# One PSUM ring for attention and FFN, and RMS weights folded into the FFN weights one group earlier

## The chip, the cores and the metric

The kernel runs on one core of one Trainium2 chip. The metric is the device time of one execution in microseconds (us), the median of several runs. Five engines work side by side, each through its own list of instructions in order: PE (matmuls, with weight loads shown as PEld), DVE, ACT, POOL, and SP, which issues transfers. POOL issues transfers as well. PE writes its results only to PSUM, which has eight banks of 128 x 512 float32 values; DVE and ACT read them from there, POOL does not.

## The reference

Inputs are q, k, v of 8 batches x 8 heads x 576 tokens x 64, a forget gate f of 8 x 8 x 576, and the FFN's weights.

```python
scores = scale * np.matmul(q, k.transpose(0, 1, 3, 2))
cum = np.cumsum(np.log(np.clip(f, 0.0001, 1.0)), axis=-1)
scores = np.where(causal, -1e9, scores + cum[..., :, None] - cum[..., None, :])
x = softmax(scores) @ v            # heads side by side: 4608 tokens x 512
xn = x / np.sqrt(np.mean(x * x, axis=-1, keepdims=True) + 1e-06) * rms_g
g = xn @ w_gate                    # 512 x 1536
out = (g * sigmoid(g) * (xn @ w_val)) @ w_out   # 1536 x 512
```

## The kernel before, in words

**Attention.** Each batch has five query blocks `qi`: four of 128 tokens and a last one (`LAST`) of 64. Queries and keys are loaded as bf16 by POOL (`load_qk`, L302; `load_qk2`, L308, for 256 tokens at once), values as float32 by POOL or SP (`load_v`, L319). Queries and keys must be turned so that the head dimension lies on the partitions: by transposing transfers on SP (`turn`, L378), or for most blocks of batches 0 and 1 by PE into a PSUM bank, emptied by DVE for q and ACT for k (`turn_pe`, L387). Values are multiplied by the decay of their key (`scale_v`, L418; L426 and L427), on DVE for batches 0 and 1, on POOL for the others.

A score tile is one query block against one key block (or two key blocks for `LAST`): eight matmuls (L451) into two PSUM banks, even heads in one and odd heads in the other. `score_block` (L439) takes two tiles at a time. ACT takes the exponential of both banks of a tile in one instruction (L469), and POOL masks the diagonal tile (L476). The score blocks form a chain in the fixed order of the list `order` (L565): blocks 0 to 3 of batch 0, those of batch 1, `LAST` of batch 0, `LAST` of batch 1, and then batch after batch. `values` (L485) multiplies probabilities with values (L498) for even and for odd heads, each into one bank, and DVE divides by the sum and moves the result to SBUF (L512, L514). `norm` (L521) squares (ACT, L530), takes the power -0.5 (POOL, L534 and L535) and scales (ACT, L542). The result is turned again: for groups 0 and 1 by PE (L550), and DVE moves it to `xT` and multiplies by the RMS weights `rgT` on the way (L556); for the other groups by a transposing transfer on SP (L560), without the multiplication.

**FFN.** A group is 512 tokens: groups 0 to 7 are the first 512 of each batch, group 8 the eight `LAST` blocks together. `gate` (L596) computes 512 columns' worth of gate and value matmuls (L605) in one bank each, then tanh on ACT (L617) and two instructions on DVE, L619 (which frees the gate bank) and L612 (which frees the value bank). Groups 0 and 1 run by pieces: one gate takes four 128-wide chunks of the hidden dimension for 128 tokens, so a block `i` of the weights (512 of the 1536 columns) is used by four gates, one for each piece `j`. Later groups take one chunk for all 512 tokens, with four matmuls of 512 columns. `project` (L624) multiplies with `w_out` (L630), in three units of four matmuls into one bank, which ACT empties (L635) and SP stores (L638).

**The RMS weights.** Since groups 0 and 1 multiply xT by `rgT` while the others do not, the weights `wg` and `wv` are multiplied by `rgT` in SBUF between groups 1 and 2. `weigh` (L339) does so for one block of each, with four instructions on DVE for wg and four for wv (L345), and has to wait until the four gates of group 1 have used the block; group 2's gates wait for it.

**The order of the work.** The program is not scheduled by hand. Each piece of work is a `Unit` with an engine, an estimated duration, a `key` and the buffers that it takes and gives back (`Hold`). `Plan.run` (L79) simulates the engines with these durations and lets each idle engine take, of its units that are ready and whose buffers are free (`fits`, L54), the one with the lowest key; a small random number from a fixed seed is added to each key (L88). The resulting order is what each engine executes. The group number is the FFN's key: gates of group g have keys from g to g + 0.69, its projections from g + 1.03. `akey` (L235) gives the attention of batch b from 2 on keys from b - 1.3 to b - 0.45; batches 0 and 1 have negative keys (`qkey`, L569). The due times of `load` at L663 hold loads of batches 2 and later back until certain gates have begun.

**PSUM.** Three rings share the eight banks: `sc`, two slots of two banks, for scores; `po`, one bank, for values; `ff`, three banks, for turns, gates, projections and the odd heads of batch 0's values. When the last score (or value) has been planned, its slots pass to `ff` (`heir`, L69). Rings not named in the set at L207 are handed out to whichever unit runs first, and `sc`, `po` and `ff` are not named there.

Of the kernel before, what the change touches and what calls it, by code (L numbers as in the profile page):

```python
# [32 lines left out]
class Plan:  # L33
# [3 lines left out]
    def __init__(self, rings, fifo, heir):  # L37
        self.units, self.fifo, self.heir = [], fifo, heir
        self.free = {name: list(range(n)) for name, n in rings.items()}
        self.left = {name: [] for name in rings}  # L40
# [106 lines left out]
def fox_ffn_kernel(ctx, tc, q, k, v, f, moe_w_gate, moe_w_val, moe_w_out, moe_rms_g, out):  # L147
# [15 lines left out]
    def ring(name, n, shape, dt, pool=sb):  # L163
# [3 lines left out]
                 sc=2, po=1, ff=3, hw=8, sw=8)  # L167
# [38 lines left out]

    P = Plan(sizes, {"v32", "qk", "qk2", "QT", "Vs", "PT", "x", "xn"}, {"sc": ("ff", lambda i: [n_ff + 2 * i, n_ff + 2 * i + 1]),  # L207
                     "po": ("ff", lambda i: [n_ff + 2 * n_sc + i])})
# [25 lines left out]

    def akey(b, w):  # L235
        return b - 1 - LEAD + SPAN * w
# [20 lines left out]
    iden_f = pool(0.7, -15.5, emit_ident)  # L257
# [20 lines left out]
    h_dec = Hold("ff", 1 + EARLY)  # L278

    def emit_dect():  # L280
        for j in range(NB):
            nc.tensor.transpose(T_ff[h_dec.slot][:, j * 64:(j + 1) * 64], dec[:, j * 128:(j + 1) * 128],
                                ident_f[0:BH, 0:BH])
# [3 lines left out]
        decT, T_ff[h_dec.slot][:, 0:NB * 64].rearrange("p (j b) -> p j b", b=BH)), [d5], give=[h_dec])  # L287
# [44 lines left out]
    def load_w(i, key):  # L332
        c0, c1 = i * 512, (i + 1) * 512
        for w, src, nm in ((wg, moe_w_gate, "g"), (wv, moe_w_val, "v")):
            def emit(w=w, src=src):
                nc.gpsimd.dma_start(out=w[:, :, c0:c1], in_=src[:, c0:c1].rearrange("(c p) f -> p c f", p=128))
            Lw[nm, i] = load("POOL", 0.75, (512, 0.0061), key, emit, late=2.6)

    def weigh(i, key, deps):  # L339

        c0, c1 = i * 512, (i + 1) * 512
        for w, nm in ((wg, "g"), (wv, "v")):
# [3 lines left out]
            Lw[nm, i] = dve(1.14, key, emit, deps)  # L346
# [40 lines left out]
    def turn_pe(b, j, two, key):  # L387

        t0, r_of = j * 128, 2 if two else 1
        for dst, nm, add, cp in ((T_QT, "q", dve, nc.vector.tensor_copy), (T_KT, "k", act, nc.scalar.copy)):  # L390
            hq, h = hold_qk[b, nm, j], Hold("ff", 1)

            def emit(hq=hq, h=h):
                tp = T_ff[h.slot].bitcast(BF16)
# [12 lines left out]
            def copy(dst=dst, h=h, cp=cp):  # L407
                tp = T_ff[h.slot].bitcast(BF16)[:, 0:512 * r_of].rearrange("p (c r t) -> p c r t", r=r_of, t=128)
# [9 lines left out]
    def scale_v(b, j, key):  # L418
# [3 lines left out]
        def emit(eng):  # L422
            dj = decT[0:n, j, b * H:(b + 1) * H]
            if early:
                dj = T_ff[h_dec.slot][0:n, j * 64:j * 64 + H]
# [10 lines left out]

    hold_PT, masked, last_block = {}, {}, [None]

    def score_block(tiles, key):  # L439

        holds = [Hold("sc", 1) for _ in tiles]

        def emit():
            for (b, qi, kjs, n), h in zip(tiles, holds):
                kt, qt, t = T_KT[hold_QT[b].slot], T_QT[hold_QT[b].slot], T_sc[h.slot]
# [12 lines left out]
        u = pe(0.19 + 0.24 * cols, key, emit, deps, take=holds, give=gives)  # L458
        last_block[0] = u
        for (b, qi, kjs, n), h in zip(tiles, holds):  # L460
# [7 lines left out]
            def ex(h=h, hp=hp, cols=cols, T_of_p=T_of_p, half=half):  # L468
                nc.scalar.activation(T_of_p[hp.slot][:, 0:2 * half].rearrange("p (a c) -> p a c", a=2)[:, :, 0:cols],  # L469
                                     T_sc[h.slot][:, :, 0:cols], ACT.Exp, scale=scale)  # L470
            e = act(0.2 + 0.82 * cols / 512, key, ex, [u], take=[hp], give=[h])
# [8 lines left out]
    def bank_of(h):  # L480
        return T_ff[h.slot] if h.ring == "ff" else T_po[h.slot]

    hold_x, evac, last_val = {}, {}, [None]

    def values(b, qi, key):  # L485
        p0, n = rows(qi)
        hx = hold_x[b, qi] = Hold("x", 1)
        for par in range(2):
            hpo = Hold("ff" if b == 0 and par == 1 and qi < LAST else "po", 1)

            def emit(par=par, hpo=hpo):
                po = bank_of(hpo)[:, 0:4 * 65].rearrange("p (j d) -> p j d", d=65)
# [16 lines left out]
            def ev(par=par, hpo=hpo):  # L509
                po = bank_of(hpo)[0:n, 0:4 * 65].rearrange("p (j d) -> p j d", d=65)  # L510
# [10 lines left out]
    def norm(b, js, key):  # L521
# [15 lines left out]
        for i, j in enumerate(js):  # L537
# [6 lines left out]
            if g < 2:  # L544
                hf = Hold("ff", 1)

                def tr(hn=hn, hf=hf):
                    tp = T_ff[hf.slot].bitcast(BF16)
# [5 lines left out]
                def cp(hf=hf, g=g, c=c):  # L554
                    tp = T_ff[hf.slot].bitcast(BF16)[:, 0:512].rearrange("p (c t) -> p c t", t=128)
                    nc.vector.tensor_tensor(T_of[g][hold_xT[g].slot][:, :, c:c + 128], tp, bcast(rgT, 128), ALU.mult)  # L556
                pieces[b, j] = dve(0.65, key - 0.02, cp, [t, L_rg], take=[hold_xT[g]], give=[hf])
# [38 lines left out]
    def gate(g, key, deps, i, pairs):  # L596

        hg, hv, ht, ha = Hold("ff", 1), Hold("ff", 1), Hold("th", 1), Hold("ga", 1)
        hx = hold_xT[g]

        def mm(w, h):
            xT = T_of[g][hx.slot]
            for fc, t0, n, c in pairs:
                for dc in range(NDC):
                    nc.tensor.matmul(T_ff[h.slot][:, c:c + n], lhsT=w[:, dc, fc * 128:(fc + 1) * 128],  # L605
                                     rhs=xT[:, dc, t0:t0 + n], start=(dc == 0), stop=(dc == NDC - 1))

        def last():
            fc, t0, n, c = pairs[0]
            hT = T_hT[hold_hT[g].slot][:, fc:fc + len(pairs), t0:t0 + n]  # L610
            three = [t.rearrange("p (f t) -> p f t", t=n) for t in (T_ga[ha.slot], T_ff[hv.slot])]
# [5 lines left out]
        th = act(0.6, key - 0.1, lambda: nc.scalar.activation(T_th[ht.slot], T_ff[hg.slot], ACT.Tanh, scale=0.5),  # L617
                 [ug], take=[ht])
        a = dve(0.72, key - 0.1, lambda: nc.vector.scalar_tensor_tensor(  # L619
            T_ga[ha.slot], in0=T_th[ht.slot], scalar=1.0, in1=T_ff[hg.slot], op0=ALU.add, op1=ALU.mult),  # L620
# [3 lines left out]
    def project(g, j, key):  # L624
        hf, ho = Hold("ff", 1), Hold("ores", 1)
        last = None
        for part in range(3):
            def emit(part=part):
                for fc in range(part * 4, part * 4 + 4):
                    nc.tensor.matmul(T_ff[hf.slot], lhsT=T_hT[hold_hT[g].slot][:, fc, j * 128:(j + 1) * 128],  # L630
# [4 lines left out]
        c = act(0.59, key - 0.05, lambda: nc.scalar.copy(T_ores[ho.slot], T_ff[hf.slot]), [last], take=[ho], give=[hf])  # L635
# [12 lines left out]
    for g in range(G):  # L648
        if g < 2:
            for i in range(3):  # L650
# [4 lines left out]
                if g == 1:  # L655
                    weigh(i, 1 + (i * 4 + 4) / 16, [ended[1, i * 4 + j] for j in range(4)])
# [54 lines left out]
```

## Time and profile before

| | |
|---|---|
| median of 3 runs | 400.06 us (399.75 to 400.39) |
| profiled execution | 398.83 us |
| its span, first to last instruction | 396.7 us |
| mean granted TensorE clock | 0.984 |
| PE, DVE, ACT, POOL busy | 92%, 57%, 60%, 50% of the span |
| moved | 44.83 MB |

A row of the profile names line, engine, operation, `out<-in` by the names of the program's tiles with buffer numbers left out, shapes and the count. In rows of groups, the first number behind the bar is busy time in us and the second the mean duration of one in ns; what follows is idle time of the engine just before them and what ended it. In the timeline the first two numbers are start and duration in us, and the bracket holds the idle time before and what ended it. In rows of waits, "a <- b" says that a waited for b, in us in total, how many times, and the longest. A busy PE is not a PE at its peak, since the ends of matmuls are modelled.

### The profile page before, as it was taken

Reading aid. Unit: us, or ns where it says so; the run is one execution under the profiler, and the core shown is the slowest. Engines: PE = TensorE matmul, PEld = TensorE weight load, DVE = VectorE, ACT = ScalarE, POOL = GpSimd, SP = SyncE. Lnnn points to the kernel's source line nnn. Section 1 sums busy time; section 2 is a strip of 40 time slices with the busy share of each in tenths; the row PEclk is TensorE's granted clock in tenths of the full one; section 3 lists DMA queues with packets and bytes.
Section 4 is the critical chain, followed back from the end, with each engine's and each line's share of the span. In section 5 each row is a group of like instructions: output and inputs, shape, how many; then the busy total and the mean of one; then the engine's idle time right before and its main releaser. Section 6 shows DMA issues by size and latency. Waiting matters only on the chain.

```text
span 396.7 us, 9672 instructions
## 1 busy us (share of the span) xinstructions
PE 365.8 (92%) x3941; PEld 217.4 (55%) x3941; DVE 225.0 (57%) x456; ACT 237.7 (60%) x377; POOL 196.8 (50%) x275
## 2 busy tenths in 40 slices
PE   2668999997699999899999999999999999999995
PEld 1567898785496554554455544554555444444442
DVE  4555787478968555564565555645555554455530
ACT  4655588786647955786677657865885532232212
POOL 8862469997839945695398456841211100000000
PEclk9998999999979999999999999999999999999998
DMA  9999999999829999899799999992120210001004
GB/s 132 189 200 190 199 143 162 176 175 168 141 39 109 187 158 122 103 154 154 78 122 168 161 112 82 190 150 55 32 57 28 55 33 28 26 26 55 26 28 106
DMA packets 133708, 44.83 MB, mean 113 GB/s; under 512 B 122432, under 2 KB 127040, under 8 KB 133664
## 3 DMA queue, kind: packets, MB, share of 16 engines
q0 software_dynamic: 76000, 22.16, 59.2%
q1 hardware_dynamic: 57136, 22.05, 30.7%
q8 instruction: 31, 0.51, 0.6%
q10 hardware_dynamic: 528, 0.00, 0.2%
q14 instruction: 13, 0.11, 0.1%
HBM read 37.90 MB, written 9.44 MB: 119 GB/s over the span
## 4 chain that ended last, share of the span: by engine, by line
PE 78%; DMA 7%; DVE 7%; POOL 4%; issue 2%; ACT 1%; SPq 0%; ACTq 0%; POOLq 0%
PE ff L605 35%; PE ff L630 17%; PE po L498 7%; PE sc L605 6%; PE sc L451 6%; PE sc L630 5%; DMA v<-in_v_dram 4%; DMA xT<-xn 3%; PE po L605 2%; DVE wg L345 1%; DVE wv L345 1%; DVE hT L612 1%; DVE ga L619 1%; POOL qk L303 1%; DVE x L514 1%
## 5 line engine op out<-in xcount | busy, mean ns | idle before, releaser
L469 ACT ACTIVATE PT<-sc 128x1024 bf16<-128x1024 f32 x96 | 95.2, 1018 | 22.6 <-PE sc L451 22.5
L605 PE MATMUL ff<-xT,wg 128*128 128x128 bf16 (+1 forms) x628 | 88.8, 290 | 5.9 <-DVE ga L619 3.2
L605 PE MATMUL ff<-xT,wv 128*128 128x128 bf16 (+1 forms) x636 | 90.7, 288 | 1.0 <-DVE hT L612 0.8
L619 DVE SCALAR_TENSOR_TENSOR ga<-th,ff 128x512 f32<-128x512 f32 x87 | 59.2, 683 | 49.2 <-ACT th L617 48.8
L630 PE MATMUL ff<-wo,hT 128*128 128x512 bf16 x336 | 86.1, 379 | 0.0
L605 PEld LDWEIGHTS <-wg 128*128 128x128 bf16 x720 | 55.9, 102 | 42.4 <-issue 6.3
L617 ACT ACTIVATE th<-ff 128x512 f32<-128x512 f32 x87 | 51.5, 595 | 44.6 <-PE ff L605 32.8
L605 PEld LDWEIGHTS <-wv 128*128 128x128 bf16 x720 | 54.9, 100 | 36.6 <-issue 1.8
L612 DVE SCALAR_TENSOR_TENSOR hT<-ga,ff 128x512 bf16<-128x512 f32 x94 | 63.7, 683 | 18.7 <-PE ff L605 16.7
L630 PEld LDWEIGHTS <-hT 128*128 128x128 bf16 x432 | 40.1, 98 | 45.1 <-issue 1.3
L476 POOL TENSOR_SCALAR_AFFINE_SELECT PT<-PT 128x1024 bf16<-128x1024 bf16 x32 | 35.4, 1106 | 58.0 <-ACT PT L469 57.7
L498 PEld LDWEIGHTS <-PT 128*128 128x128 bf16 x896 | 38.4, 99 | 17.3 <-issue 4.8
L498 PE MATMUL po<-Vs,PT 128*128 128x65 bf16 x856 | 41.1, 196 | 3.2 <-DVE x L514 2.4
L426 POOL TENSOR_TENSOR Vs<-v,decT 128x512 bf16<-128x512 f32 (+1 forms) x30 | 31.7, 1057 | 12.8 <-DMA v<-in_v_dram 12.2
L451 PE MATMUL sc<-QT,KT 64*128 64x128 bf16 (+1 forms) x960 | 34.6, 214 | 3.0 <-ACT PT L469 1.4
L512 DVE RECIPROCAL rden<-po 128x4 f32<-128x4 f32 (+1 forms) x76 | 13.5, 177 | 40.7 <-PE po L498 40.5
L451 PEld LDWEIGHTS <-KT 64*128 64x128 bf16 x960 | 25.0, 97 | 19.4 <-issue 14.9
L530 ACT ACTIVATE junk<-x 128x512 bf16<-128x512 f32 (+1 forms) x40 | 25.1, 627 | 14.7 <-DVE x L514 14.6
L514 DVE TENSOR_TENSOR x<-po,rden 128x256 f32<-128x256 f32 (+1 forms) x76 | 32.1, 423 | 2.6
L326 POOL DMA_DIRECT2D v<-in_v_dram x34 | 30.4, 896 | 0.1
L303 POOL DMA_DIRECT2D qk<-in_q_dram x34 | 30.1, 885 | 0.8 <-POOLq L695 0.8
L542 ACT ACTIVATE xn<-x,rs 128x512 bf16<-128x512 f32 (+1 forms) x40 | 27.2, 714 | 5.4 <-POOL rs L535 5.3
(76 smaller groups left out, 306.1 us busy)
## 6 DMA issues: line engine op xcount, KB each, us to landing
out_dram<-ores SPq DMA_DIRECT2D x32, 256.0 KB, 2.4
v<-in_v_dram POOLq DMA_DIRECT2D x27, 256.0 KB, 5.3
qk<-in_q_dram POOLq DMA_DIRECT2D x26, 128.0 KB, 5.9
qk<-in_k_dram POOLq DMA_DIRECT2D x26, 128.0 KB, 5.7
wg<-in_moe_w_gate_dram POOLq DMA_DIRECT2D x3, 512.0 KB, 15.9
wv<-in_moe_w_val_dram POOLq DMA_DIRECT2D x3, 512.0 KB, 17.4
wo<-in_moe_w_out_dram POOLq DMA_DIRECT2D x2, 768.0 KB, 17.6
v<-in_v_dram SPq DMA_DIRECT2D x5, 256.0 KB, 9.9
```

What stands on the lines that cost most here:

```text
L303: nc.gpsimd.dma_start(out=T_qk[h.slot][0:n, :].rearrange("p (h d) -> p h d", d=D), in_=src[b, :, p0:p0 + n, :].rearrange("h p d -> p h d"))
L426: eng.tensor_tensor(T_Vs[hv.slot][0:n, j, :, 0:D], T_v32[h.slot][0:n, :, :], bcast(dj, D), ALU.mult)
L451: nc.tensor.matmul(t[:, par, c:c + n], lhsT=kt[r, p, kj * 128:(kj + 1) * 128], rhs=qt[r, p, qi * 128:qi * 128 + n], start=True, stop=True)
L469: nc.scalar.activation(T_of_p[hp.slot][:, 0:2 * half].rearrange("p (a c) -> p a c", a=2)[:, :, 0:cols], T_sc[h.slot][:, :, 0:cols], ACT.Ex ...
L476: nc.gpsimd.affine_select(out=d, in_=d, pattern=[[0, 8], [1, n]], compare_op=ALU.is_ge, fill=0.0, base=0, channel_multiplier=-1)
L498: nc.tensor.matmul(po[:, p, :], lhsT=T_of_p[h.slot][:, c:c + 128], rhs=vs[:, kj, 2 * p + par, :], start=(kj == 0), stop=(kj == qi))
L514: nc.vector.tensor_tensor(d, po[:, :, 0:D], bcast(r, D), ALU.mult)
L605: nc.tensor.matmul(T_ff[h.slot][:, c:c + n], lhsT=w[:, dc, fc * 128:(fc + 1) * 128], rhs=xT[:, dc, t0:t0 + n], start=(dc == 0), stop=(dc = ...
L612: nc.vector.scalar_tensor_tensor(hT, in0=three[0], scalar=0.5, in1=three[1], op0=ALU.mult, op1=ALU.mult)
L617: th = act(0.6, key - 0.1, lambda: nc.scalar.activation(T_th[ht.slot], T_ff[hg.slot], ACT.Tanh, scale=0.5), [ug], take=[ht])
L619: a = dve(0.72, key - 0.1, lambda: nc.vector.scalar_tensor_tensor(T_ga[ha.slot], in0=T_th[ht.slot], scalar=1.0, in1=T_ff[hg.slot], op0=ALU ...
L630: nc.tensor.matmul(T_ff[hf.slot], lhsT=T_hT[hold_hT[g].slot][:, fc, j * 128:(j + 1) * 128], rhs=wo[:, fc, :], start=(fc == 0), stop=(fc == ...
```

## The change

All eight banks become one tile `banks` and one ring `bank`, for scores, values, turns, projections and gates alike. A score tile takes any two banks, and its view steps from the lower to the higher of them. The rule of inheritance goes, as do the three rings.

Group 0 alone is multiplied by `rgT` in xT (`PLAIN = 1`); group 1's pieces are copied. `weigh` runs between groups 0 and 1: wg of a block once the four gate halves of group 0 on it are done, wv once the value halves are. All gates from group 1 on wait for the weighed block. The key of the weighing is 0.25 below that of the first gate which needs it, and its estimated duration is 1.3 us for four instructions instead of 1.14.

The identity matrix for PE's transposes is made on POOL behind the loads of key -15 instead of ahead of them. The attention of the `LAST` blocks of batches 0 and 1 gets keys 0.3 and 0.9 instead of -4.8 and -4.2. The seed of the small random numbers is 5 instead of 71.

The core of the diff (the replacement of `T_ff`, `T_po` and `T_sc` by `T_bank` in `turn_pe`, `gate`, `project`, `norm` and at the decay's transpose is left out):

```diff
@@ Plan
-                if h.ring in self.heir and not self.left[h.ring]:
-                    to, slots = self.heir[h.ring]
-                    self.free[to] += slots(h.slot)
-                else:
-                    self.free[h.ring].append(h.slot)
+                self.free[h.ring].append(h.slot)
...
-        draw = random.Random(71)
+        draw = random.Random(5)
@@ fox_ffn_kernel
-                 sc=2, po=1, ff=3, hw=8, sw=8)
+                 bank=8, hw=8, sw=8)
...
-    T_sc = ring("sc", sizes["sc"], [128, 2, 512], F32, ps)
-    T_po = ring("po", sizes["po"], [128, 512], F32, ps)
-    T_ff = ring("ff", sizes["ff"], [128, GT], F32, ps)
-    n_ff, n_sc = sizes["ff"], sizes["sc"]
-    T_ff += [t[:, i, :] for t in T_sc for i in range(2)] + T_po
+    banks = ps.tile([128, sizes["bank"], 512], F32, name="banks")
+    T_bank = [banks[:, i, :] for i in range(sizes["bank"])]
...
+    PLAIN = 1
...
-    iden_f = pool(0.7, -15.5, emit_ident)
+    iden_f = pool(0.7, -14.5, emit_ident)
@@ weigh
-            Lw[nm, i] = dve(1.14, key, emit, deps)
+            Lw[nm, i] = [dve(1.3, key, emit, deps[nm])]
@@ score_block
+    def two_banks(h):
+        a, z = sorted(x.slot for x in h)
+        return banks[:, a:z + 1:z - a, :]
...
-        holds = [Hold("sc", 1) for _ in tiles]
+        holds = [(Hold("bank", 1), Hold("bank", 1)) for _ in tiles]
...
-                                     T_sc[h.slot][:, :, 0:cols], ACT.Exp, scale=scale)
+                                     two_banks(h)[:, :, 0:cols], ACT.Exp, scale=scale)
@@ values
-            hpo = Hold("ff" if b == 0 and par == 1 and qi < LAST else "po", 1)
+            hpo = Hold("bank", 1)
@@ norm
-                    nc.vector.tensor_tensor(T_of[g][hold_xT[g].slot][:, :, c:c + 128], tp, bcast(rgT, 128), ALU.mult)
-                pieces[b, j] = dve(0.65, key - 0.02, cp, [t, L_rg], take=[hold_xT[g]], give=[hf])
+                    to = T_of[g][hold_xT[g].slot][:, :, c:c + 128]
+                    if g < PLAIN:
+                        nc.vector.tensor_tensor(to, tp, bcast(rgT, 128), ALU.mult)
+                    else:
+                        nc.vector.tensor_copy(to, tp)
+                pieces[b, j] = dve(0.69 if g < PLAIN else 0.42, key - 0.02, cp, [t, L_rg], take=[hold_xT[g]], give=[hf])
@@ qkey
-            return (2 * b - 9 + 0.2 * (START[qi] + ahead)) if qi < LAST else -4.8 + 0.6 * b + 0.04 * ahead
+            return (2 * b - 9 + 0.2 * (START[qi] + ahead)) if qi < LAST else 0.3 + 0.6 * b + 0.04 * ahead
@@ gate
-        began[g, len([x for x in began if x[0] == g])] = ug = pe(dur, key, lambda: mm(wg, hg), deps + [Lw["g", i]], take=[hg])
-        uv = pe(dur, key + 0.0001, lambda: mm(wv, hv), [ug, Lw["v", i]], take=[hv], give=[hx])
+        began[g, len([x for x in began if x[0] == g])] = ug = pe(dur, key, lambda: mm(wg, hg), deps + Lw["g", i], take=[hg])
+        uv = pe(dur, key + 0.0001, lambda: mm(wv, hv), [ug] + Lw["v", i], take=[hv], give=[hx])
@@ groups
-                if g == 1:
-                    weigh(i, 1 + (i * 4 + 4) / 16, [ended[1, i * 4 + j] for j in range(4)])
+                if g == PLAIN - 1:
+                    weigh(i, PLAIN - 1 + (i * 4 + 12) / 16, {"g": [began[g, i * 4 + j] for j in range(4)],
+                                                            "v": [ended[g, i * 4 + j] for j in range(4)]})
```

More of the change, by code (lines that the diff above doesn't have):

```diff
@@ L277, in fox_ffn_kernel @@
     EARLY = 3
-    h_dec = Hold("ff", 1 + EARLY)
+    h_dec = Hold("bank", 1 + EARLY)
     def emit_dect():
         for j in range(NB):
-            nc.tensor.transpose(T_ff[h_dec.slot][:, j * 64:(j + 1) * 64], dec[:, j * 128:(j + 1) * 128],
+            nc.tensor.transpose(T_bank[h_dec.slot][:, j * 64:(j + 1) * 64], dec[:, j * 128:(j + 1) * 128],
                                 ident_f[0:BH, 0:BH])
@@ L286, in fox_ffn_kernel @@
     L_dec = dve(0.45, -19, lambda: nc.vector.tensor_copy(
-        decT, T_ff[h_dec.slot][:, 0:NB * 64].rearrange("p (j b) -> p j b", b=BH)), [d5], give=[h_dec])
+        decT, T_bank[h_dec.slot][:, 0:NB * 64].rearrange("p (j b) -> p j b", b=BH)), [d5], give=[h_dec])
     def rows(j):
@@ L336, in emit @@
                 nc.gpsimd.dma_start(out=w[:, :, c0:c1], in_=src[:, c0:c1].rearrange("(c p) f -> p c f", p=128))
-            Lw[nm, i] = load("POOL", 0.75, (512, 0.0061), key, emit, late=2.6)
+            Lw[nm, i] = [load("POOL", 0.75, (512, 0.0061), key, emit, late=2.6)]
     def weigh(i, key, deps):
@@ L390, in turn_pe @@
         for dst, nm, add, cp in ((T_QT, "q", dve, nc.vector.tensor_copy), (T_KT, "k", act, nc.scalar.copy)):
-            hq, h = hold_qk[b, nm, j], Hold("ff", 1)
+            hq, h = hold_qk[b, nm, j], Hold("bank", 1)
             def emit(hq=hq, h=h):
-                tp = T_ff[h.slot].bitcast(BF16)
+                tp = T_bank[h.slot].bitcast(BF16)
                 for p in range(4):
@@ L457, in score_block @@
         cols = sum(len(kjs) * n / 128 for b, qi, kjs, n in tiles)
-        u = pe(0.19 + 0.24 * cols, key, emit, deps, take=holds, give=gives)
+        u = pe(0.19 + 0.24 * cols, key, emit, deps, take=[x for h in holds for x in h], give=gives)
         last_block[0] = u
@@ L469, in ex @@
                 nc.scalar.activation(T_of_p[hp.slot][:, 0:2 * half].rearrange("p (a c) -> p a c", a=2)[:, :, 0:cols],
-                                     T_sc[h.slot][:, :, 0:cols], ACT.Exp, scale=scale)
-            e = act(0.2 + 0.82 * cols / 512, key, ex, [u], take=[hp], give=[h])
+                                     two_banks(h)[:, :, 0:cols], ACT.Exp, scale=scale)
+            e = act(0.2 + 0.82 * cols / 512, key, ex, [u], take=[hp], give=h)
             masked.setdefault((b, qi), []).append(e)
@@ L478, in score_block @@
                 masked[b, qi].append(pool(0.15 + 0.95 * n / 128, key, mk, [e]))
-    def bank_of(h):
-        return T_ff[h.slot] if h.ring == "ff" else T_po[h.slot]
     hold_x, evac, last_val = {}, {}, [None]
@@ L544, in norm @@
             if g < 2:
-                hf = Hold("ff", 1)
+                hf = Hold("bank", 1)
                 def tr(hn=hn, hf=hf):
-                    tp = T_ff[hf.slot].bitcast(BF16)
+                    tp = T_bank[hf.slot].bitcast(BF16)
                     for dc in range(NDC):
@@ L596, in gate @@
     def gate(g, key, deps, i, pairs):
-        hg, hv, ht, ha = Hold("ff", 1), Hold("ff", 1), Hold("th", 1), Hold("ga", 1)
+        hg, hv, ht, ha = Hold("bank", 1), Hold("bank", 1), Hold("th", 1), Hold("ga", 1)
         hx = hold_xT[g]
@@ L624, in project @@
     def project(g, j, key):
-        hf, ho = Hold("ff", 1), Hold("ores", 1)
+        hf, ho = Hold("bank", 1), Hold("ores", 1)
         last = None
@@ L634, in project @@
                       give=[hold_hT[g]] if part == 2 else [])
-        c = act(0.59, key - 0.05, lambda: nc.scalar.copy(T_ores[ho.slot], T_ff[hf.slot]), [last], take=[ho], give=[hf])
+        c = act(0.59, key - 0.05, lambda: nc.scalar.copy(T_ores[ho.slot], T_bank[hf.slot]), [last], take=[ho], give=[hf])
         if g < B:
```

29 lines of the change are left out of this document (14 added, 15 removed).

## The prediction, as it was recorded

> **What bounds the kernel now.** First the page's busy times and its chain, then busy time by stage (columns: length of the stretch, then PE, PEld, DVE, ACT, POOL busy us with instruction counts, the granted TensorE clock, DMA share, GB/s).
>
> ```profile
> PE 365.8 (92%) x3941; PEld 217.4 (55%) x3941; DVE 225.0 (57%) x456; ACT 237.7 (60%) x377; POOL 196.8 (50%) x275
> PE 78%; DMA 7%; DVE 7%; POOL 4%; issue 2%; ACT 1%; SPq 0%; ACTq 0%; POOLq 0%
> ```
> ```profile
> 0.00:20.00 20.00, 9.09 (x117) 6.68 (x117) 10.33 (x39) 10.86 (x14) 17.20 (x27) 1.00 1.24 161
> 20.00:40.00 20.00, 15.19 (x224) 14.06 (x225) 11.77 (x28) 11.00 (x18) 8.94 (x13) 0.91 1.34 195
> 40.00:60.00 20.00, 19.25 (x396) 18.06 (x392) 16.11 (x28) 14.49 (x21) 11.28 (x14) 1.00 1.39 170
> 60.00:80.00 20.00, 19.11 (x370) 15.07 (x365) 11.98 (x28) 16.87 (x29) 19.04 (x28) 1.00 1.91 165
> 80.00:120.00 40.00, 33.81 (x581) 28.83 (x581) 30.99 (x56) 25.68 (x42) 28.51 (x41) 0.91 1.06 133
> 120.00:390.00 270.00, 267.54 (x2264) 134.05 (x2262) 143.83 (x281) 157.66 (x256) 111.81 (x156) 1.00 0.73 92
> ```
>
> PE is the bound, and from 120 to 390 us it is full: 270 − 267.54 = 2.5 us idle in 270. Nothing large is to be had there. What PE loses lies in front: 10.9 us idle before 20, when the first loads arrive; 4.8 between 20 and 40, with a clock of 0.91 that costs 0.09 × 15.19 = 1.4 more; 0.75 and 0.9 in the next two stages; and between 80 and 120 6.2 idle plus 0.09 × 33.81 = 3.0 by the clock, **9.2 us**. This last stage holds the multiplication of the FFN weights by the RMS weights (L345, between groups 1 and 2). Who ended PE's waits there (columns: total, times, longest):
>
> ```profile
> PE ff L605 <- DVE ga L619: 3.2, 1, 3.2
> PE po L498 <- DVE x L514: 2.4, 3, 1.6
> ```
>
> PE waits for PSUM banks that DVE should have emptied, and DVE is in the weighing. Its instructions on one block of wg, and those that ran later (columns: duration min/median/max in ns, first and last start):
>
> ```profile
> L345 DVE TENSOR_SCALAR wg<-wg,rgT x4: 332/1105/4528, 101.0 to 107.5; 128x512 bf16<-128x512 bf16 x4
> ```
> ```profile
> L345 DVE TENSOR_SCALAR wv<-wv,rgT x8: 336/338/340, 108.3 to 121.6; 128x512 bf16<-128x512 bf16 x8
> ```
>
> The same instruction takes 0.34 us or 4.53. The long one is no work but a wait, while POOL went from one computation to the next; its largest group between 101 and 105.5 is
>
> ```profile
> L426 POOL TENSOR_TENSOR Vs<-v,decT 128x512 bf16<-128x512 f32 x3 | 3.2, 1055 | 0.0
> ```
>
> **The change part by part.**
>
> *Weighing a group earlier.* It takes away the weighing between 80 and 125: 24 instructions.
>
> ```profile
> L345 DVE TENSOR_SCALAR wg<-wg,rgT 128x512 bf16<-128x512 bf16 x12 | 10.9, 968 | 0.0
> L345 DVE TENSOR_SCALAR wv<-wv,rgT 128x512 bf16<-128x512 bf16 x12 | 6.0, 554 | 0.0
> ```
>
> 16.9 us of DVE leave a stage where DVE was busy 30.99 of 40. What is late next there is batch 2, whose pieces open group 2:
>
> ```profile
> 103.52 0.71 PE L498 MATMUL po<-Vs,PT 128*128 128x65 bf16 x16
> ...
> 110.67 1.04 PE L498 MATMUL po<-Vs,PT 128*128 128x65 bf16 x16 [0.34 <-DVE x L514]
> ```
>
> The two halves of one values unit stand 7.15 us apart since there is one bank for them and DVE, in the wg weighing from 101.0 to 107.8, empties it late. Without the excess over four times 0.34, some 5 us come back on this path, with 1.6 at the longest wait of L498 before it and, as the gaps go, part of the clock's 3.0. Ends: 0 and −9.2. I take **−7.5**.
>
> The same 24 instructions come in again between 46 and about 80. wg of a block may be weighed once the four gate matmuls of group 0 have read it, wv likewise. Counting gates, these rows are the first gate that could read group 0's last piece, group 0's last gate and group 1's first:
>
> ```profile
> 44.90 1.05 PE L605 MATMUL ff<-xT,wg 128*128 128x128 bf16 x16
> ...
> 61.41 1.05 PE L605 MATMUL ff<-xT,wv 128*128 128x128 bf16 x16
> ...
> 66.36 1.06 PE L605 MATMUL ff<-xT,wg 128*128 128x128 bf16 x16
> ```
>
> So block 0 is free at about 47 and is wanted at 66.36: 19 us for 8 × 0.34 = 2.7. Block 2 is free at 62.5 and wanted last. The new wait sits on PE ahead of group 1's gates, with attention, projections and everything else of PE behind it; it is covered by those 19 us. DVE is the question. It was busy 16.11 of 20 before 60 and 11.98 of 20 after; 24 at 0.34, 8.2 us, fit into 3.9 + 8.0 free, 16.9 don't. POOL decides, and what it does then is this:
>
> ```profile
> L303 POOL DMA_DIRECT2D qk<-in_k_dram x7 | 6.2, 890 | 0.0
> L476 POOL TENSOR_SCALAR_AFFINE_SELECT PT<-PT 128x1024 bf16<-128x1024 bf16 x4 | 4.5, 1131 | 7.5 <-ACT PT L469 7.5
> ```
>
> That is POOL from 46 to 76: mostly load issues, and few computations, each alone. If each of those four holds one weigh for its 1.13 us, DVE pays 8.2 + 4.5 = 12.7, just more than the 11.9 free. PE has little slack before 60 (0.75 idle), so I take **+1.5**; ends 0 and +9.2, as much as the old stage lost.
>
> The Trainium skill, page "SBUF — State Buffer", section "Who interferes with whom", says that VectorE in its two-port modes and GpSimd hold one port pair by turns, each for a whole instruction, and that descriptor writing for GpSimd's own loads needs it too. By that rule the load issues of 46 to 76 hold a weigh up as a computation does, about 0.9 each, and the term would be nearer its upper end, which is the first rival below. The trace agrees only in part: 4.53 us spans several POOL instructions, not one, and of the eight short ones the last four, from 120.9, ran at 336 to 340 ns beside POOL's load issues, which themselves came slower:
>
> ```profile
> 120.94 2.40 POOL L303 DMA_DIRECT2D qk<-in_q_dram  x2
> ```
>
> *Group 1's pieces as plain copies.*
>
> ```profile
> L556 DVE TENSOR_TENSOR xT<-ff,rgT 128x512 bf16<-128x512 bf16 x8 | 5.4, 689 | 3.9 <-PE ff L550 3.9
> ```
> ```profile
> L410 DVE COPY QT<-ff 128x512 bf16<-128x512 bf16 x2 | 0.8, 410 | 0.0
> ```
>
> Four instructions, 0.28 each, 1.1 us of DVE, not on PE's path: **0** (ends −1.1 and 0).
>
> *One ring of eight banks.* Instructions stay the same; waits for a bank change. The two longest of PE that the ring could end, before the weighing, are:
>
> ```profile
> PE ff L498 <- DVE ga L619: 1.5, 1, 1.5
> PE sc L451 <- ACT PT L469: 1.4, 2, 1.1
> ```
>
> 2.9 us in all. Loads are late next:
>
> ```profile
> DVE Vs L426 <- DMA v<-in_v_dram: 4.5, 3, 2.8
> ```
>
> so half of it: **−1.5** (ends −2.9 and 0). From 120 on at most the 2.5 idle are to be had: **0**; the loss that is possible there is a rival. Exponentials now read two banks that may lie apart; no row shows it. Nearest is L469 on adjacent ones:
>
> ```profile
> L469 ACT ACTIVATE PT<-sc 128x1024 bf16<-128x1024 f32 x96 | 95.2, 1018 | 22.6 <-PE sc L451 22.5
> ```
>
> I take the same 1018 ns, **0**; the end on the bad side is the rival on order below.
>
> *Identity after four load issues.*
>
> ```profile
> 3.61 0.29 POOL masks.py:199 TENSOR_SCALAR_AFFINE_SELECT ident_f<-ident_f 128x128 f32<-128x128 f32 x1
> ...
> 12.47 1.20 POOL L476 TENSOR_SCALAR_AFFINE_SELECT PT<-PT 128x1024 bf16<-128x1024 bf16 x1
> ```
> ```profile
> PE ff L397 <- DMA qk<-in_q_dram: 5.5, 1, 5.5
> ```
>
> Identity comes four issues, some 3.6 us, later, at about 7.5 instead of 3.9; the four loads come 0.6 earlier. PE's first turns, at 5.5 now, wait 2 us for it, but the first mask waits on POOL behind load issues until 12.47 in any case: **0** (−0.6 to +1).
>
> *The 64-row blocks of batches 0 and 1 at keys 0.3 and 0.9.* Score blocks go in a fixed chain, and these follow batch 1's; group 0's gates were over by 62.5 and group 1's have keys from 1.0, so their place on PE stays. Later are their transposes on SP, their DVE scalings, and so two v buffers, with batch 2's v loads behind them on POOL. Those are scaled only when the old values are out,
>
> ```profile
> 76.54 1.04 POOL L426 TENSOR_TENSOR Vs<-v,decT 128x512 bf16<-128x512 f32 x1 [0.41 <-PE po L498]
> ```
>
> so there is cover; I take **+0.5** (0 to +2). The new draw of the keys reorders near-equals: 0, ±2, the size of one or two of the waits above.
>
> **The sum** is −7.5 + 1.5 − 1.5 + 0.5 = −7.0. The profiled run took 398.83 (span 396.7): 391.8. The median of 400.06 lies 1.23 above it, so **393.1**.
>
> **Rivals.** *The stall only moves.* POOL's load issues and masks hold the weighing in 46–80 as its computations did in 80–120; DVE, 80% busy before 60, falls behind, and PE, with 0.75 us of slack, pays the whole +9.2: 393.1 − 1.5 + 9.2 = 400.8. For it: PE full there. Against: the 336 to 340 ns beside load issues. *Scores starve.* A pair of score tiles needs four free banks at one moment, a gate or projection only one; whatever comes free goes to the FFN. The chain has group 2's first 512-wide gate, one such unit, as
>
> ```profile
> 123.57 0.86 PE ff L605 x4
> ```
>
> If each of a batch's seven score blocks loses one unit of 0.86 us, its pieces come 6 us later. It decides from the point at which pieces land after PE has used up the group before, and two group starts stood near it:
>
> ```profile
> PE ff L605 <- DMA xT<-xn: 1.8, 2, 1.2
> ```
>
> At 2 us for each of groups 2 to 7, +12: 405, slower. *Separate banks are ordered as a span.* If the wait between an exponential and the matmuls covers the banks between its two, PE waits for L469 not 1.4 us but at half of some 52 pairs of tiles (13 tiles in each of 8 batches), about 0.8 of the 1.018 each: +20, 413, and the change does not do what it says. *The ring gives all.* −2.9 instead of −1.5, all of the 2.5, no new cost of the weighing's +1.5 and the +0.5: 387.2.
>
> **How the numbers follow.** Forecast 0.57 (389 to 398 around 393.1), ring gives all 0.08, stall moves 0.15, starving 0.14, span 0.06. Measurement tells 0.2% apart, 0.8 us. Faster: 0.57 + 0.08 + 0.05 of the moved stall = 0.70; same 0.04 of it; slower 0.06 of it + 0.14 + 0.06 = 0.26. The range 386.5 to 402 leaves out the span, most of starving, and little below.
>
> **What would show it.** Right: L345 between 46 and 80, nearer 8 us than 17; PE over 37 of 40 between 80 and 120 at a clock near 1; group 2's first 512-wide gate some 6 us earlier than 123.6. Wrong: DVE full between 46 and 66 with PE idle behind it; PE waiting at group starts for xT; PE waits for L469 of tens of us.

## The result, and the profile after

The changed kernel takes **426.12 us** (median of 4 runs, 423.16 to 428.12) against 400.07 before: a ratio of 1.0645, with a 95% interval of 1.0568 to 1.0723. The forecast was 393.1, in a range from 386.5 to 402. The profiled execution has a span of 422.6 us. Busy time by stage, in the columns of the prediction:

```profile
0.00:20.00 20.00, 8.47 (x117) 6.95 (x117) 10.75 (x37) 11.17 (x13) 16.28 (x27) 1.00 1.29 167
20.00:40.00 20.00, 13.71 (x184) 12.80 (x185) 8.57 (x21) 10.43 (x17) 9.00 (x12) 0.83 1.35 195
40.00:60.00 20.00, 17.48 (x335) 16.30 (x331) 16.30 (x30) 10.28 (x15) 7.06 (x10) 0.94 1.18 157
60.00:80.00 20.00, 17.73 (x303) 14.00 (x301) 16.85 (x39) 14.30 (x22) 14.74 (x17) 0.98 1.11 106
80.00:120.00 40.00, 35.64 (x701) 30.55 (x699) 22.84 (x57) 30.33 (x49) 33.81 (x51) 1.00 1.36 149
120.00:390.00 270.00, 247.15 (x2191) 125.07 (x2189) 133.81 (x261) 154.07 (x250) 115.79 (x161) 1.00 0.72 91
```

The stage of the old weighing did get better: PE 35.64 instead of 33.81 of 40, at a clock of 1.00 instead of 0.91. But the long stage behind it, where PE had 2.5 us idle, now has 270 − 247.15 = **22.9**, and the stages before 80 lost some 7.6 us: 5.3 of PE's busy time, and 2.4 by the lower clock, counted as the prediction counts it. So the loss is spread over the whole attention and does not sit at one place. Among the waits of PE and DVE that are new, or much longer than before, the longest six name one engine and one line, the exponential; a seventh row makes PE's waits for it complete but for 0.6 us:

```profile
DVE rden L506 <- ACT PT L466: 12.4, 8, 2.7
DVE ga L617 <- ACT PT L466: 10.1, 7, 2.9
PE banks L603 <- ACT PT L466: 9.9, 11, 1.4
PE banks L492 <- ACT PT L466: 9.9, 11, 1.1
PE banks L448 <- ACT PT L466: 9.3, 9, 2.0
DVE hT L610 <- ACT PT L466: 9.1, 9, 1.7
PE banks L628 <- ACT PT L466: 4.1, 3, 1.8
```

Before, PE waited 1.4 us for it in all, and only for the next scores. Here gates (L603), values (L492), scores (L448) and projections (L628) wait, and even DVE, none of whose three instructions uses anything that an exponential writes. The exponential itself is about as fast as before (1021 ns against 1018); what grew is the idle time ahead of it, from 22.6 us to 64.3:

```profile
L466 ACT ACTIVATE PT<-banks 128x1024 bf16<-128x1024 f32 x96 | 96.5, 1021 | 64.3 <-PE banks L448 15.0
```

One place in the timeline shows the form of it. First ACT, then PE:

```profile
175.37 0.58 ACT L633 COPY ores<-banks 128x512 f32<-128x512 f32 x1 [0.16 <-PE banks L628]
177.34 1.02 ACT L466 ACTIVATE PT<-banks 128x1024 bf16<-128x1024 f32 x1 [1.39 <-PE banks L603]
```
```profile
173.75 0.62 PE L448 MATMUL banks<-QT,KT 64*128 64x128 bf16 x16
174.30 1.04 PE L628 MATMUL banks<-wo,hT 128*128 128x512 bf16 x4
175.17 1.03 PE L603 MATMUL banks<-xT,wg 128*128 128x512 bf16 x4
176.04 0.41 PE L492 MATMUL banks<-Vs,PT 128*128 128x65 bf16 x8
176.28 1.02 PE L603 MATMUL banks<-xT,wv 128*128 128x512 bf16 x4
178.42 0.41 PE L492 MATMUL banks<-Vs,PT 128*128 128x65 bf16 x8 [1.11 <-ACT PT L466]
```

The scores that the exponential of 177.34 reads were done at 174.4. In the plan they lie in banks 2 and 7. The exponential nevertheless waits until the `wv` matmuls of 176.28 are over, the second half of a gate, which the plan has in bank 3; and the values of 178.42, planned in bank 6, wait for the exponential. The compiled program has just these two waits. Banks 3 and 6 are not the exponential's banks; they lie between them. That is the third rival of the prediction: the view from bank 2 to bank 7 (a view is the part of a tile that an instruction names) is ordered like the whole span.

### The profile page after: what moved, and what is told of

It reads as the page before. It is cut to its first block, busy times and chain, and to the rows that moved or that the text cites. A ratio compares the mean times of both kernels' runs of the same rounds, so it can differ in the third digit from the quotient of the medians.

```text
span 422.6 us, 9728 instructions
## 1 busy us (share of the span) xinstructions
PE 367.9 (87%) x3941; PEld 218.0 (52%) x3941; DVE 219.5 (52%) x456; ACT 238.3 (56%) x377; POOL 196.7 (47%) x275
## 4 chain that ended last, share of the span: by engine, by line
PE 74%; ACT 11%; DMA 7%; DVE 4%; issue 2%; POOL 1%; ACTq 0%; DVEq 0%; POOLq 0%
PE banks L603 40%; PE banks L628 21%; ACT PT L466 10%; PE banks L492 7%; PE banks L448 5%; DMA v<-in_v_dram 5%; DMA xT<-xn 2%; DVE hT L610 1%; ACT th L615 1%; DVE x L508 1%; DVE ga L617 1%; PE banks L396 1%; POOL qk L296 0%; DVE Vs L419 0%; DVE QT L403 0%
## 5 line engine op out<-in xcount | busy, mean ns | idle before, releaser
L466 ACT ACTIVATE PT<-banks 128x1024 bf16<-128x1024 f32 x96 | 96.5, 1021 | 64.3 <-PE banks L448 15.0
L617 DVE SCALAR_TENSOR_TENSOR ga<-th,banks 128x512 f32<-128x512 f32 x108 | 73.4, 685 | 87.3 <-ACT th L615 76.9
L628 PE MATMUL banks<-wo,hT 128*128 128x512 bf16 x432 | 108.9, 379 | 4.1 <-ACT PT L466 4.1
L603 PE MATMUL banks<-xT,wv 128*128 128x128 bf16 (+1 forms) x672 | 98.1, 290 | 8.3 <-ACT PT L466 7.6
L603 PE MATMUL banks<-xT,wg 128*128 128x128 bf16 (+1 forms) x672 | 99.3, 294 | 3.7 <-ACT PT L466 2.2
L615 ACT ACTIVATE th<-banks 128x512 f32<-128x512 f32 x108 | 63.6, 595 | 62.2 <-PE banks L603 58.8
L610 DVE SCALAR_TENSOR_TENSOR hT<-ga,banks 128x512 bf16<-128x512 f32 x108 | 72.5, 684 | 27.4 <-PE banks L603 16.0
L603 PEld LDWEIGHTS <-wv 128*128 128x128 bf16 x720 | 54.4, 99 | 45.7 <-issue 10.0
L603 PEld LDWEIGHTS <-wg 128*128 128x128 bf16 x720 | 55.8, 101 | 40.0 <-issue 4.8
L628 PEld LDWEIGHTS <-hT 128*128 128x128 bf16 x432 | 39.8, 98 | 47.6 <-issue 4.5
L492 PE MATMUL banks<-Vs,PT 128*128 128x65 bf16 x896 | 42.4, 196 | 12.5 <-ACT PT L466 9.9
L492 PEld LDWEIGHTS <-PT 128*128 128x128 bf16 x896 | 38.0, 99 | 29.2 <-issue 13.9
L448 PE MATMUL banks<-QT,KT 64*128 64x128 bf16 (+1 forms) x960 | 35.7, 217 | 12.6 <-ACT PT L466 9.3
L448 PEld LDWEIGHTS <-KT 64*128 64x128 bf16 x960 | 26.8, 98 | 26.5 <-issue 23.8
L508 DVE TENSOR_TENSOR x<-banks,rden 128x256 f32<-128x256 f32 (+1 forms) x80 | 33.8, 423 | 2.9 <-DVE rden L506 0.2
```

The lines of the kernel that those rows point to most:

```text
L448: nc.tensor.matmul(t[:, par, c:c + n], lhsT=kt[r, p, kj * 128:(kj + 1) * 128], rhs=qt[r, p, qi * 128:qi * 128 + n], start=True, stop=True)
L492: nc.tensor.matmul(po[:, p, :], lhsT=T_of_p[h.slot][:, c:c + 128], rhs=vs[:, kj, 2 * p + par, :], start=(kj == 0), stop=(kj == qi))
L508: nc.vector.tensor_tensor(d, po[:, :, 0:D], bcast(r, D), ALU.mult)
L603: nc.tensor.matmul(T_bank[h.slot][:, c:c + n], lhsT=w[:, dc, fc * 128:(fc + 1) * 128], rhs=xT[:, dc, t0:t0 + n], start=(dc == 0), stop=(dc ...
L628: nc.tensor.matmul(T_bank[hf.slot], lhsT=T_hT[hold_hT[g].slot][:, fc, j * 128:(j + 1) * 128], rhs=wo[:, fc, :], start=(fc == 0), stop=(fc ...
```

## The experiments

Theories. **Span**: an instruction whose view steps over banks is ordered with everything that touches a bank between. **Starving**: score tiles, which need four free banks at once, lose them to the FFN. For the rest of the change, whether the earlier weighing, the keys or the new draw does good or harm. Each ratio is to the kernel before, run again beside the version.

**Two controls on the kernel before, of one order of instructions.** All three PSUM tiles of the kernel before become one; rings, keys and order stay as they were. The layouts differ in bank numbers alone.

```diff
-    T_sc = ring("sc", sizes["sc"], [128, 2, 512], F32, ps)
-    T_po = ring("po", sizes["po"], [128, 512], F32, ps)
-    T_ff = ring("ff", sizes["ff"], [128, GT], F32, ps)
+    banks = ps.tile([128, 8, 512], F32, name="banks"); T_sc = [banks[:, a:z + 1:z - a, :] for a, z in ((0, 1), (2, 3))]
+    T_po = [banks[:, i, :] for i in (4,)]
+    T_ff = [banks[:, i, :] for i in (5, 6, 7)]
```

Near:

> The kernel before, in its own order, with its eight banks declared as one tile: scores on banks 0-1 and 2-3, values on 4, the FFN's ring on 5, 6, 7. Span theory (the waits around a view that steps over banks cover the banks between): the pairs are adjacent, nothing lies between, so the time of before, 399 to 401 us, and PE's waits for the exponential stay at 1 to 2 us. Starving theory (score tiles need four free banks of a common ring): the rings are still apart, so also 399 to 401. That one tile for all banks is itself the harm: over 405.

Measured: 398.48 us against 400.51, ratio 0.9971 (0.9935 to 1.0007): no difference shown. One tile for all banks does no harm.

Far, against near:

```diff
-    banks = ps.tile([128, 8, 512], F32, name="banks"); T_sc = [banks[:, a:z + 1:z - a, :] for a, z in ((0, 1), (2, 3))]
-    T_po = [banks[:, i, :] for i in (4,)]
-    T_ff = [banks[:, i, :] for i in (5, 6, 7)]
+    banks = ps.tile([128, 8, 512], F32, name="banks"); T_sc = [banks[:, a:z + 1:z - a, :] for a, z in ((0, 6), (1, 7))]
+    T_po = [banks[:, i, :] for i in (2,)]
+    T_ff = [banks[:, i, :] for i in (3, 4, 5)]
```

> The kernel before, in its own order, one tile, same rings; only the banks differ: the two score slots are banks 0 and 6, and 1 and 7; values on 2, the FFN's ring on 3, 4, 5. Each pair now has all other rings between. Span theory: every exponential waits for the FFN's and values' users of banks 2 to 5 and they for it, in all 104 tiles instead of 77 in the changed kernel: 420 to 445 us, waits for the exponential on PE and DVE of 40 us and more. Starving theory: nothing changes, 399 to 401.

Measured: **533.39 us**, ratio 1.3317 (1.3236 to 1.3398). The same instructions in the same order take a third longer because two pairs of banks lie far apart. The longest waits of PE and DVE for an exponential, and the exponentials, of that run:

```profile
DVE ga L619 <- ACT PT L469: 49.1, 21, 5.2
DVE hT L612 <- ACT PT L469: 47.4, 24, 4.5
PE banks L605 <- ACT PT L469: 39.5, 34, 1.9
PE banks L498 <- ACT PT L469: 36.4, 32, 1.6
DVE rden L512 <- ACT PT L469: 28.9, 15, 4.4
PE banks L630 <- ACT PT L469: 19.8, 16, 2.5
```
```profile
L469 ACT ACTIVATE PT<-banks 128x1024 bf16<-128x1024 f32 x96 | 98.3, 1024 | 147.6 <-PE banks L605 84.8
```

The pattern of the changed kernel, enlarged, and again with exponentials of 1.02 us: reading banks far apart is not slow in itself. The direction was as the span theory expects, the size was beyond its 420 to 445; all of PE's waits for exponentials in this run add up to 115 us. In the compiled programs, 94 of the 104 exponentials here carry a wait for DVE, 56 in the changed kernel and none in the near layout or before. Not all of the 56 are due to the span: of the two versions below in which no view spans other banks, the one with neighbouring pairs has 15 such waits among 104, the one with split exponentials 31 among 208.

**A middle layout**: score slots on banks 0 and 2, and 1 and 3; values on 4, FFN on 5, 6, 7. Against the near layout:

```diff
-    banks = ps.tile([128, 8, 512], F32, name="banks"); T_sc = [banks[:, a:z + 1:z - a, :] for a, z in ((0, 1), (2, 3))]
+    banks = ps.tile([128, 8, 512], F32, name="banks"); T_sc = [banks[:, a:z + 1:z - a, :] for a, z in ((0, 2), (1, 3))]
```

> The kernel before in its own order, one tile, the score slots on banks 0 and 2, and 1 and 3; values on 4, the FFN's ring on 5, 6, 7. Each slot now spans one bank of the other slot and none of the FFN's or the values'. Span theory: only the two score slots get in each other's way, and those already follow each other; well under half of the 133 us of the wide layout: 400 to 430 us, with waits for the exponential on PE's score matmuls alone and none on DVE. If two banks far apart were slow to read in themselves, exponentials would be longer than 1.02 us here and in the wide layout.

Measured: 401.24 us, ratio 1.0018 (0.9983 to 1.0053): no difference shown, at the low end of what was expected. PE's waits for the exponential are 2.9 us, all at scores, and DVE has none. Stepping over a bank costs nothing measurable here when the bank between belongs to the other score slot, which is used in turn anyway. It matters whose bank lies between.

**The changed kernel with split exponentials**, in its own order of instructions (the score matmuls, which then name their two banks one by one, are left out):

```diff
-                nc.scalar.activation(T_of_p[hp.slot][:, 0:2 * half].rearrange("p (a c) -> p a c", a=2)[:, :, 0:cols],
-                                     two_banks(h)[:, :, 0:cols], ACT.Exp, scale=scale)
+                for par, x in enumerate(sorted(y.slot for y in h)):
+                    nc.scalar.activation(T_of_p[hp.slot][:, par * half:par * half + cols], T_bank[x][:, 0:cols], ACT.Exp, scale=scale)
```

> The changed kernel in its own order, with each exponential over two banks done as two instructions of one bank each, so that no view steps over banks. Costs ACT 104 x about 0.18 us = 19 us more, of 184 us that it is idle. Span theory: the stalls on the exponential go; PE idle between 120 and 390 falls from 23 us to under 6, and the time to 398 to 408 us. Starving theory: the order and the takes of banks are the same, so no gain: 424 to 440.

Measured: **384.54 us**, ratio 0.9603 (0.9544 to 0.9663). The fastest of all kernels here, below the 398 to 408 that the span theory expected, though ACT works longer:

```profile
L467 ACT ACTIVATE PT<-banks 128x512 bf16<-128x512 f32 x192 | 100.8, 600 | 20.5 <-PE banks L448 20.4
```

An exponential of 1.02 us has become two with 100.8 us busy in all instead of 96.5 (their durations, 600 ns each, overlap). The idle time ahead of them is 20.5 us, near the 22.6 of before, and no wait of PE for an exponential is left. Busy time by stage:

```profile
20.00:40.00 20.00, 17.28 (x284) 16.40 (x284) 13.39 (x29) 12.36 (x26) 11.31 (x17) 1.00 1.34 196
40.00:60.00 20.00, 19.56 (x382) 17.45 (x383) 19.72 (x39) 16.31 (x31) 10.89 (x14) 1.00 1.56 179
60.00:80.00 20.00, 19.55 (x386) 16.00 (x384) 18.31 (x45) 16.22 (x36) 19.32 (x27) 1.00 1.69 168
80.00:120.00 40.00, 39.30 (x640) 29.18 (x638) 20.53 (x50) 32.67 (x70) 35.91 (x51) 1.00 1.53 164
120.00:370.00 250.00, 249.04 (x2111) 125.27 (x2109) 136.63 (x258) 150.57 (x300) 102.38 (x144) 1.00 0.69 93
```

PE idles 1 us in 250, with the same order and the same takes of banks as the changed kernel. Starving is refuted as the cause: it would still be there. Two things in the runs fit its coming out so far below what was expected: the ring is worth more than was thought, and splitting costs ACT less (both below).

**The changed kernel with neighbouring pairs**, one exponential per tile. Single banks are taken, where possible, from pairs already broken (the lines for that are left out):

```diff
+    def pairs(self, ring):
+        free = set(self.free[ring])
+        return [a for a in sorted(free) if a % 2 == 0 and a + 1 in free]
...
-        a, z = sorted(x.slot for x in h)
-        return banks[:, a:z + 1:z - a, :]
+        return banks[:, h.slot:h.slot + 2, :]
```

> The changed kernel, but a score tile takes an aligned pair of neighbouring banks (0-1, 2-3, 4-5, 6-7) and single takers prefer a bank whose neighbour is already taken. One exponential per tile as before; nothing lies between its banks. The order is planned anew. Span theory: no stalls on the exponential; near the split version (384.5), a little behind because pairs are harder to find than any two banks: 384 to 394 us. If it was starving after all, pairs starve more: over 400.

Measured: 391.35 us (385.67 to 395.39), ratio 0.9831 (0.9753 to 0.9908). PE's waits for the exponential are 0.3 us. So the second way to avoid the span also removes the loss. It was planned anew, and its runs scatter more, so that the difference to 384.54 is not put down to the pairs alone.

**The rest of the change on the three rings of before.** Against the kernel before, with the changed kernel's weighing and its plain copy of later pieces (`PLAIN = 1`) beside these lines:

```diff
-        draw = random.Random(71)
+        draw = random.Random(5)
-    iden_f = pool(0.7, -15.5, emit_ident)
+    iden_f = pool(0.7, -14.5, emit_ident)
-            return (2 * b - 9 + 0.2 * (START[qi] + ahead)) if qi < LAST else -4.8 + 0.6 * b + 0.04 * ahead
+            return (2 * b - 9 + 0.2 * (START[qi] + ahead)) if qi < LAST else 0.3 + 0.6 * b + 0.04 * ahead
```

> The rest of the change without the ring: weighing between groups 0 and 1, plain copies for group 1, the later identity, the keys 0.3 and 0.9 and the new seed, on the three rings of before. Span theory and starving theory alike put all of the loss on the ring: this kernel should then show the prediction's other steps, 391 to 397 us. If the weighing, the keys or the seed did the harm: over 405.

Measured: 392.62 us, ratio 0.9819 (0.9746 to 0.9892), as expected. So the ring of eight, as written, cost all of the 26 us and more: 426.1 − 392.6 = 33.5. But which part saved the 8?

**The earlier weighing alone**, on the kernel before, with its draw, keys and identity:

```diff
-                if g == 1:
-                    weigh(i, 1 + (i * 4 + 4) / 16, [ended[1, i * 4 + j] for j in range(4)])
+                if g == PLAIN - 1:
+                    weigh(i, PLAIN - 1 + (i * 4 + 12) / 16, {"g": [began[g, i * 4 + j] for j in range(4)],
+                                                            "v": [ended[g, i * 4 + j] for j in range(4)]})
```

> The kernel before with the weighing moved between groups 0 and 1 and plain copies for group 1, and nothing else (three rings, old keys, old seed, early identity). If the weighing is what the three-ring version gained: 391 to 395 us, with PE near full between 80 and 120. If keys, seed or identity brought it: 397 to 401.

Measured: 400.48 us, ratio 1.0033 (0.9998 to 1.0069): nothing gained. Its stages:

```profile
40.00:60.00 20.00, 17.31 (x320) 15.83 (x317) 16.36 (x32) 12.82 (x18) 9.20 (x12) 0.91 1.38 170
60.00:80.00 20.00, 17.14 (x398) 15.01 (x396) 17.68 (x43) 15.83 (x26) 18.83 (x25) 1.00 1.62 148
80.00:120.00 40.00, 36.96 (x620) 30.20 (x618) 20.86 (x44) 29.23 (x47) 31.08 (x47) 1.00 1.27 137
```

Between 80 and 120 PE has 3.2 us more and the full clock; between 40 and 80 it has 3.9 less and a clock of 0.91 for half of it. Counting the clock as the prediction does, these are about 6.2 us gained and 5.5 lost. DVE shows one of the waits behind the loss:

```profile
55.72 2.27 DVE L347 TENSOR_SCALAR wv<-wv,rgT 128x512 bf16<-128x512 bf16 x4
57.91 0.16 DVE L514 RECIPROCAL rden<-po 128x4 f32<-128x4 f32 x1
58.11 0.42 DVE L516 TENSOR_TENSOR x<-po,rden 128x256 f32<-128x256 f32 x1
```
```profile
58.59 0.40 PE L500 MATMUL po<-Vs,PT 128*128 128x65 bf16 x8 [1.13 <-DVE x L516]
```

The old stall in small: values wait for the one values bank behind a weighing, now at 58 instead of 108. This is 1.1 us; the rest of the loss is not followed wait by wait.

**The three-ring version with the old seed:**

```diff
-        draw = random.Random(5)
+        draw = random.Random(71)
```

> The three-ring version (392.6 us) with the old seed 71, all else of it kept: earlier weighing, keys 0.3 and 0.9, late identity. The earlier weighing alone gave 400.5. If the keys of the 64-row blocks (or the late identity) brought the 8 us: 391 to 395. If the new draw of the small random numbers brought them: 398 to 402.

Measured: 400.6 us, ratio 1.0001 (0.9962 to 1.0041).

**The three-ring version with the old keys:**

```diff
-            return (2 * b - 9 + 0.2 * (START[qi] + ahead)) if qi < LAST else 0.3 + 0.6 * b + 0.04 * ahead
+            return (2 * b - 9 + 0.2 * (START[qi] + ahead)) if qi < LAST else -4.8 + 0.6 * b + 0.04 * ahead
```

> The three-ring version with the old keys -4.8 and -4.2, all else of it kept. If the keys brought the 8 us: 398 to 402. If the draw (or the late identity) brought them: 391 to 395.

Measured: 391.87 us, ratio 0.977 (0.9729 to 0.9811). The keys of the 64-row blocks do nothing measurable; with the weighing early, the draw of the small random numbers does.

**Keys, seed and late identity without the earlier weighing**: the three pairs of lines of the three-ring diff, alone, on the kernel before.

> The kernel before with keys, seed and late identity of the change, three rings, and the weighing still between groups 1 and 2. If keys, seed and identity save the time by themselves: 391 to 395 us. If they only pay because they make room on DVE for the earlier weighing: 398 to 403, with PE's losses between 80 and 120 as before.

Measured: 398.12 us, ratio 0.9985 (0.9907 to 1.0064). No gain of these three without the earlier weighing is shown; the interval leaves room for 0.9% at most. In these runs the 8 us come only with both, draw and weighing: the weighing frees the stage from 80 to 120, and the order of the new draw keeps PE busy in the stages that the weighing moved into. Here are these stages of the three-ring version, and below them the same with the old seed:

```profile
40.00:60.00 20.00, 19.56 (x366) 18.44 (x365) 17.54 (x39) 13.77 (x20) 8.87 (x12) 0.91 1.35 161
60.00:80.00 20.00, 18.77 (x396) 15.78 (x391) 17.13 (x42) 17.17 (x29) 19.68 (x26) 1.00 2.19 133
```
```profile
40.00:60.00 20.00, 15.69 (x292) 14.08 (x292) 14.67 (x33) 12.70 (x18) 10.37 (x13) 0.91 1.41 165
60.00:80.00 20.00, 15.99 (x349) 14.53 (x344) 15.91 (x37) 14.86 (x24) 16.00 (x21) 0.91 1.86 144
```

Two draws were tried, so this is what one order did, not a property of any draw.

**The ring alone, with split exponentials**: against the split version, the weighing, keys, seed and identity are those of before (shown are the lines of the weighing).

```diff
-    PLAIN = 1
+    PLAIN = 2
...
-                    weigh(i, PLAIN - 1 + (i * 4 + 12) / 16, {"g": [began[g, i * 4 + j] for j in range(4)],
+                    weigh(i, PLAIN - 1 + (i * 4 + 4) / 16, {"g": [ended[g, i * 4 + j] for j in range(4)],
```

> The kernel before with the ring of eight banks alone, exponentials split so that no view spans other banks; weighing, keys, seed and identity as before. The prediction gave the ring 1.5 us, at most 5.4; the split version against the three-ring one says 8. If the ring's worth stands by itself: 391 to 394 us. If it only pays together with the earlier weighing, which fills DVE where banks are short: 397 to 401.

Measured: 391.13 us, ratio 0.9787 (0.9748 to 0.9827). Without the span the ring is worth some 8 us by itself, as much as between the three-ring version and the split one (392.6 − 384.5).

**The split version with the identity made early again:**

```diff
-    iden_f = pool(0.7, -14.5, emit_ident)
+    iden_f = pool(0.7, -15.5, emit_ident)
```

> The split version (384.5 us) with the identity matrix made ahead of the four load issues again; the order is planned anew. PE's first turn then starts at about 5.5 us instead of 7.7. If that start is on the path: 382 to 384. If the first mask and the loads set the pace, as the prediction had it: 384 to 386; more only by another order.

Measured: 388.31 us, ratio 0.971 (0.9647 to 0.9774). PE's first turn starts 2 us sooner and the kernel is no faster; the order was planned anew, and with it the rest moved too. Neither a loss nor a gain by the late identity is shown, since order and place changed together.

## Why the prediction was wrong, point by point

**The ring: the step that failed.** The prediction wrote "Instructions stay the same; waits for a bank change" and then listed only waits that the ring could end. For the exponential it compared durations ("I take the same 1018 ns, **0**"), which was right, 1021, and put the added waits into a rival of 0.06. That rival is what happened, and the sign that the prediction gave for it, waits of PE for L469 of tens of us, is in the profile. It had been priced at 20 us, by PE's waits alone. PE's own waits for exponentials measured 33.8 us, since there were more of them than 26, and each lasted about 1 us and not 0.8. The split version, with the same order, puts the whole price at 426.1 − 384.5 = 41.6. What lies beyond PE's own waits is put down to ACT and DVE, which wait as well, and to the work that queues on ACT behind a late exponential; that part is argued. 77 of the 104 tiles had drawn banks that were not neighbours. The warning was in the diff: a view with a step that depends on which banks are free.

**The ring's worth** was put at −1.5, at best −2.9 and 2.5 later on. Without the span it is about −8 (0.9787). The prediction counted only PE's listed waits for a bank before the weighing. A likely reason, which no run isolates: in three rings PE's order is planned around banks that are not free, and this shows as a fuller or emptier stage and as a lowered clock, not as a wait for a bank. Between 20 and 40 the split version has PE at 17.28 and a clock of 1.00; the three-ring version, with the same weighing, keys and draw, has 14.64 and 0.91.

**The weighing: the mechanism right, one size not.** Its instructions did become short: in the changed kernel

```profile
L338 DVE TENSOR_SCALAR wg<-wg,rgT x12: 333/344/1832, 59.6 to 84.0; 128x512 bf16<-128x512 bf16 x12
```

instead of 4528 at the longest. Moved alone, with the draw of before, all of it took DVE 12.2 us, next to the 12.7 that the prediction worked out:

```profile
L347 DVE TENSOR_SCALAR wg<-wg,rgT 128x512 bf16<-128x512 bf16 x12 | 5.8, 541 | 0.0
L347 DVE TENSOR_SCALAR wv<-wv,rgT 128x512 bf16<-128x512 bf16 x12 | 6.4, 591 | 0.0
```

But −7.5 + 1.5 was wrong with that draw: measured 0, near what the first rival ("the stall only moves") says. By the stages, the −7.5 was about −6.2, and the +1.5 was about +5.5: that is the term mis-sized. DVE's time was foreseen, and what its delay costs PE was not.

**The draw** was given 0, ±2. Of the two draws tried, one is 8 us faster than the other once the weighing is early. **Keys**: +0.5 forecast, nothing measurable. **Identity**: 0 forecast; PE's first turn waited until 7.7 as worked out, and no loss was shown. **Starving**, 0.14, refuted. The three-ring version came out at 392.6, next to the forecast, but that is luck: it has no ring of eight, the terms of the weighing and of the draw were wrong, and the weighing's gain needed the draw.

## What to carry to other kernels

When a change lets one instruction read several buffers that are handed out separately, ask what else will be ordered with it: the order kept may cover all that lies between. A layout test with the same instructions in the same order and other bank numbers separates this from theories of scheduling, with two runs. And a step that moves work into a full stage needs a price of its own there: here one stage gained about 6.2 us and the two before it lost about 5.5.

## What the runs showed of the hardware that was not expected

An exponential over 1024 columns takes 1018 ns in the mean where its two banks are neighbours, 1019 where they are two apart (0 and 2) and 1024 where they are six apart. What costs is the order that the compiled program keeps around it, not the reading.

Two exponentials of one bank each take 600 ns in the records, but 192 of them were busy for 100.8 us, against 95.2 (before) and 96.5 (changed) for 96 of double size. The records overlap, so splitting cost ACT some 4 to 6 us, not the 19 that adding durations gave.
